# An attention and spectral mixing kernel: the last segment's scores in full-width units, and a new written-out order of all engines' work

## The chip, the cores and the metric

The kernel runs on one core of a Trainium2 chip. A core has a matrix engine (TensorE, PE in the profile, with PEld for its weight loads), a vector engine (VectorE, DVE), an activation engine (ScalarE, ACT), GpSimd (POOL) and SyncE (SP), which here only issues DMA transfers. The engines run side by side, each through its own queue in order, and wait for one another by semaphores. The metric is device time in microseconds (us); lower is better. Before the change the median of three runs is 236.53 us (235.4 to 236.88).

## What is computed

Two branches over the same input x (2048 tokens by 640 features, bf16) are mixed by a sigmoid gate per token. Branch A is attention with 32 heads of 20 features over four segments of 512 tokens. Each segment has causal softmax attention inside itself, and reads from a memory (M, z) that sums the segments before it. Branch B is a two-dimensional Fourier transform, a product with a complex weight, and the inverse transform.

```
for s in range(N):                       # N = 4 segments of L = 512
    qs, ks, vs = (q[:, :, s].copy(), k[:, :, s].copy(), v[:, :, s].copy())
    logits = jnp.einsum('bhqd,bhkd->bhqk', qs, ks) * scale + mask
    p = _softmax(logits, axis=-1)
    a_dot = jnp.einsum('bhqk,bhkd->bhqd', p, vs)
    pq = phi(qs)                         # t + 1 where t > 0, else exp(t)
    a_mem = num / den                    # pq with M, pq with z
    o = g * a_mem + (1.0 - g) * a_dot
    pk = phi(ks)
    M = M + jnp.einsum('bhld,bhle->bhde', pk, vs)
    z = z + jnp.einsum('bhld->bhd', pk)
...
X = rfft2(x); y = irfft2(X * (w_r + 1j * w_i))
out = g * (o @ wo) + (1 - g) * y         # g = sigmoid(sum(x * gate_w))
```

## The kernel before

Everything lies in one program that writes out each engine's instructions. `record` lists the operations with what they read and write; from that come the waits. The order in which each engine runs them is not found when the kernel is built: it stands in the list `ORDER` (L639). An entry is twice the operation's number, plus one where the operation has two engines to choose from and takes the second. `Sched.schedule` deals the entries out to five queues, so `ORDER` sets the order within TensorE, VectorE, ScalarE, GpSimd and SyncE, and which engine a copy (`copy_alts`) or a sum (`either`) runs on. A transfer in SyncE's queue that waits holds all transfers behind it.

Scores. For each segment the 32 heads are eight groups of four (g), two groups a pair (`pr`). The triangle of 512 by 512 scores is split in three kinds of unit, each of which fills four banks of PSUM (2048 columns a partition), is run by `qk_unit` on TensorE in a row-tiled array mode (`mode=1`), and is then exponentiated by ScalarE into the tile `ex`. Kind 0 and kind 1 hold one head group each; kind 2 gathers the small pieces that are left, 128 columns a head. In segments 1 and 2 (`wide`, L1256) a unit of kind 2 gathers those of four groups, every second pair; in segments 0 and 3 it gathers two groups, once in every pair (`UNITS`). Segment 3 has a layout of its own in `ex` (a pitch of 1280 per head where the others have 1088, `exo`, L1317): its exps of kind 1 are written in two parts of 1280 and 768 elements, and those of kind 2 in two parts of 512 (L1352 to L1362).

GpSimd clears what the causal mask forbids (`masks`, `mask`, L1407). In segments 0 to 2 the values are multiplied in a column-tiled mode (`pv_flipped`, `mode=2`), stored in DRAM (`u_scr`), and read back for the output projection. In segment 3 `pv_group` uses the exponentials as weights (L1431 and after), VectorE normalizes (`pv_den`, `pv_rec`, `pv_mul`, L1443 to L1448), the memory term in `mem` is added (`addmem`, L1453), and `last_transposes` turns the result round on TensorE.

Memory. Segments 1 and 2 store what they read from the memory in DRAM (`o_scr`); eight DMA transposes (name `oT`, L600) bring it back as `mT`, four per segment, and `finish_tile` adds them (L1670). `Macc` is the running memory.

Spectral branch. Stages F1, D, T, Tb and Db on TensorE run between the attention parts; Db's results are copied (`ev_Db`, tile `eo`) and summed into `G` (L1617).

Output. `finish_tile` does each of 16 tiles of 128 tokens in two halves: a product of `G` with the gate table `fbg` (Fb, column-tiled), then five output projections into the same bank, and a copy to `ot`, which is stored. The gate table of a segment comes from `gate_table`: a load of `gbc` and one product (L1093). A projection with `mode=-1` is flexible: it is run column-tiled as four products (L565) where its bank is held in that mode. `FLAT` names the halves that are run flat instead.

Array modes of TensorE are thus three: 0 (flat), 1 (row-tiled scores), 2 (column-tiled).

## Time and profile before

| | |
|---|---|
| median of three runs | 236.53 us (235.4 to 236.88) |
| profiled execution | 236.15 us |
| its span, first to last instruction | 234.1 us |
| instructions | 10363 |
| granted TensorE clock | 1.000 |
| moved by DMA | 42.18 MB, mean 180 GB/s |

The span is the time from the first to the last instruction of the profiled execution; 2.05 us lie around it. Views of the trace: the page begins with each engine's busy time. The chain of waits goes back from the last instruction to what released each step. The windows give busy time by stretch. Groups of instructions carry their line, engine, operation, what is written from what (`ex<-psum`), shape, count, busy time and mean length in ns, then the idle time before them. The lines of waits read: who waited, for whom, total us, times, longest. A helper's line stands for many places: L567 and L565 are all matrix products, L602 and L600 all transfers and all DMA transposes, L577 and L579 all copies on ScalarE and VectorE.

### The profile page before, as it was taken

How to read it: one execution, taken by the hardware profiler on the slowest of the kernel's cores; microseconds unless marked ns; L12 is line 12 of the kernel's file. 1: busy time of each engine (PE TensorE's matmuls, PEld its weight loads, DVE VectorE, ACT ScalarE, POOL GpSimd, SP SyncE). 2: the span in 40 equal slices, each digit the busy share in tenths (PEclk: the TensorE clock that was granted, in tenths of full speed). 3: DMA queues.
4: the chain of work that ended last, by engine and by line, in shares of the span. 5: the costliest groups of instructions: out<-in, count | busy, mean ns of one | idle time of the engine just before them, and what ended most of it. 6: DMA issues, size and time to landing. Idle time of an engine off the chain costs nothing.

```text
span 234.1 us, 10363 instructions
## 1 busy us (share of the span) xinstructions
PE 222.8 (95%) x4377; PEld 141.1 (60%) x4391; DVE 190.5 (81%) x483; ACT 196.6 (84%) x231; POOL 152.7 (65%) x303
## 2 busy tenths in 40 slices
PE   7799999999999999999999999999999999999994
PEld 2575676676555666555557545556545467667783
DVE  0389998799999896899999998999799984925564
ACT  2189888888999899999999889999999889898820
POOL 8133138365777777476796467587989677597920
PEclk9999999999999999999999999999999999999999
DMA  7999859999989457968664788577968638416224
GB/s 149 285 345 259 232 152 170 198 224 213 206 193 191 107 161 205 232 127 211 174 168 125 208 238 209 148 204 223 208 166 223 183 108 145 121 34 178 80 88 113
DMA packets 59266, 42.18 MB, mean 180 GB/s; under 512 B 30229, under 2 KB 55381, under 8 KB 59221
## 3 DMA queue, kind: packets, MB, share of 16 engines
q1 hardware_dynamic: 58180, 40.96, 75.1%
q8 instruction: 34, 0.56, 1.0%
q10 hardware_dynamic: 1040, 0.57, 0.9%
q14 instruction: 12, 0.09, 0.1%
HBM read 23.32 MB, written 12.30 MB: 152 GB/s over the span
## 4 chain that ended last, share of the span: by engine, by line
PE 70%; DVE 13%; DMA 7%; ACT 3%; SPq 2%; issue 2%; POOL 1%; DVEq 0%
PE psum L567 62%; PE psum L565 8%; DMA wk<-in_A_wk_dram 3%; DVE Pt L1563 3%; ACT ex L1370 2%; DMA pkn<-phk 2%; DVE G L1617 2%; DMA qkp<-qk_scr 2%; SPq L600 2%; DVE mem L1228 1%; DVE va L1186 1%; DVE ub L579 1%; DVE dnr L1293 1%; DVE dn L1226 1%; DVE Cp L579 1%
## 5 line engine op out<-in xcount | busy, mean ns | idle before, releaser
L1407 POOL TENSOR_SCALAR_AFFINE_SELECT ex<-ex 128x256 bf16<-128x256 bf16 (+3 forms) x224 | 104.2, 484 | 36.8 <-ACT ex L1370 6.9
L1370 ACT ACTIVATE ex<-psum 128x2048 bf16<-128x2048 f32 (+1 forms) x56 | 101.7, 1816 | 6.9 <-PE psum L567 5.5
L1361 ACT ACTIVATE ex<-psum 128x1280 bf16<-128x1280 f32 (+3 forms) x32 | 36.2, 1130 | 5.0 <-PE psum L567 4.4
L567 PE MATMUL psum<-qkp 20*64 20x64 bf16 (+5 forms) x1280 | 32.1, 270 | 1.5 <-ACT ex L1370 0.8
L567 PE MATMUL psum<-xT,wk 128*128 128x256 bf16 (+1 forms) x280 | 32.5, 273 | 0.4 <-DMA wk<-in_A_wk_dram 0.2
L567 PE MATMUL psum<-xT,wq 128*128 128x512 bf16 (+1 forms) x121 | 28.3, 380 | 2.2 <-DMA xT<-in_A_x_dram 1.7
L567 PE MATMUL psum<-wv,xT 128*32 128x321 bf16 (+3 forms) x385 | 26.4, 301 | 0.0
L1563 DVE TENSOR_TENSOR Pt<-psum,Wt 128x642 bf16<-128x642 f32 x32 | 25.6, 822 | 0.4
L567 PEld LDWEIGHTS psum<-xT,wk 128*128 128x128 bf16 (+1 forms) x280 | 20.0, 97 | 7.2 <-issue 1.5
L567 PEld LDWEIGHTS psum<-qkp 20*64 20x64 bf16 x1280 | 13.5, 103 | 17.5 <-ACT ex L1370 10.2
L976 POOL TENSOR_TENSOR xsb<-xf 128x320 bf16<-128x320 bf16 (+2 forms) x11 | 8.1, 743 | 19.8 <-DVE xf L971 10.8
L565 PE MATMUL psum<-wo,oU 128*32 128x320 bf16 x460 | 20.6, 300 | 0.0
L567 PE MATMUL psum<-big,Cp 128*128 128x321 bf16 (+1 forms) x96 | 19.0, 303 | 0.5 <-DVE G L1617 0.2
L567 PE MATMUL psum<-big,Ac 128*128 128x161 bf16 (+2 forms) x96 | 18.3, 258 | 0.4 <-DVE va L1186 0.2
L579 DVE CAST ot<-psum 128x320 bf16<-128x320 f32 x16 | 7.5, 491 | 13.0 <-PE psum L565 9.9
L567 PEld LDWEIGHTS psum<-wv,xT 128*32 128x32 bf16 (+1 forms) x385 | 13.4, 96 | 6.7 <-issue 1.4
L567 PE MATMUL psum<-ex,va 128*32 128x64 bf16 (+3 forms) x576 | 17.2, 256 | 0.3 <-ACT qu L577 0.3
L1617 DVE TENSOR_TENSOR G<-eo,psum 128x320 bf16<-128x320 f32 x32 | 15.0, 480 | 2.9 <-PE psum L567 2.6
L1186 DVE TENSOR_TENSOR va<-psum,ebx 128x320 bf16<-128x320 f32 x32 | 15.3, 486 | 2.2 <-PE psum L567 1.0
L567 PE MATMUL psum<-tt,Yt 128*128 128x256 bf16 (+1 forms) x96 | 16.2, 275 | 0.7 <-DVE Yt L1568 0.2
L567 PEld LDWEIGHTS psum<-ex,va 128*32 128x32 bf16 x576 | 10.8, 96 | 8.6 <-POOL ex L1407 1.5
L1143 ACT ACTIVATE et<-qu 128x512 bf16<-128x512 bf16 x25 | 15.7, 626 | 0.0
(106 smaller groups left out, 408.6 us busy)
## 6 DMA issues: line engine op xcount, KB each, us to landing
qkp<-qk_scr SPq DMA_DIRECT2D x28, 160.0 KB
tt<-tab_tt SPq DMA_DIRECT2D x8, 512.0 KB, 4.5
qk_scr<-qu SPq DMA_DIRECT2D x12, 256.0 KB, 3.6
u_scr<-ub SPq DMA_DIRECT2D x12, 256.0 KB, 3.5
xsb<-in_A_x_dram SPq DMA_DIRECT2D x8, 320.0 KB, 6.1
oU<-u_scr SPq DMA_DIRECT2D x15, 128.0 KB, 3.7
out_dram<-ot SPq DMA_DIRECT2D x12, 160.0 KB
Wt<-in_B_w_r_dram SPq DMA_DIRECT2D x16, 80.2 KB, 2.6
```

The source lines that it names most:

```text
L565: h = e.matmul(dst, wt, r_, start=st, stop=sp_, **{**kw, "tile_position": (0, q), "skip_group_check": True})
L567: h = e.matmul(o_, l_, r_, start=st, stop=sp_, **kw)
L579: alts["dve"] = (lambda e: e.tensor_copy(dst(), src()), 67 + 1.04 * n, 68.0)
L600: return e.dma_start_transpose(d_, s_)
L976: self.either(lambda e, dst=dst, src=src, d0=d0, n=n, op=op: e.tensor_tensor(xs.ap(o + dst, [D, 2], [1, n]), xf.ap(src + d0, [321, 2], [1, ...
L1143: self.one("act", lambda e: e.activation(et.ap(0, [1, L]), qsl(), ACT.Exp), L, [qb], [b("et", pi_)], late, fix=95, name="phi_exp")
L1186: self.one("dve", lambda e: e.tensor_tensor(va.ap(i * H * VW + h0 * VW, [VW, nh], [1, DH]), self.ps(bank, 0, [DH, nh], [1, DH]), self.ebx. ...
L1361: self.one("act", lambda e, d=d, q=q: e.activation(self.ex.ap(*d), self.ps(bank, *q), ACT.Exp, scale=SC), (2048, (1280, 768)[x], 512)[kind ...
L1370: self.one("act", lambda e, d=d, q=q: e.activation(self.ex.ap(*d), self.ps(bank, *q), ACT.Exp, scale=SC), 2048 if kind < 2 else 512 * n, [ ...
L1407: self.one("pool", lambda e: e.affine_select(self.ex.ap(*d, p0=p0, np_=np_), self.ex.ap(*q, p0=p0, np_=np_), [[0, 4], [1, n]], ALU.is_ge, ...
L1563: self.one("dve", lambda e, ri=ri, Pt=Pt, Wt=Wt, wo_=wo_, bank=bank: e.tensor_tensor(Pt.ap(ri * 322, [644, 2], [1, KD]), self.ps(bank, 0, ...
L1617: self.one("dve", lambda e, q=q, n2=n2, bank=bank, eo=eo: e.tensor_tensor(self.G.ap(n2 * D + 639 * q, [1 - 2 * q, 320]), eo.ap(q, [1, 320] ...
```

## The change

- `wide` is true for segment 3 and for the second half (two pairs) of segment 0, so that their kind 2 units gather four head groups.
- Segment 3 takes the layout of the other segments (`exo`, `EPITCH`). Its exps are written whole, one per unit. The small pieces of groups 4 to 7 and a new piece of `ex` (`X2COL`, keys x2 and x2c, one block of 128 columns per head in three turns) take over SBUF that `ub` and `Macc` had; the first writer there waits for their users (`home`, and `after` in `mask`).
- The masks of segment 3 are as many as before, three per group on the small pieces; two of the seven write out of place into the new piece.
- `pv_group` takes its weights from the new places and waits for the new keys.
- `FLAT` names one other half tile.
- `ORDER` is replaced: its first entries differ by the operations' new numbers alone, then they stand in another order. It has 2311 entries, 2329 before. In it the eight `oT` transposes come at entries 120, 161, 164, 172, 183, 191, 195 and 196 of SyncE's 239; before at 160, 161, 171, 181, 185, 188, 206 and 218. The gate store and gate load of the last segment come at 222 and 227; before at 207 and 219. Some operations change engine, among them four `ev_Db` copies from ScalarE to VectorE and four `addmem` from GpSimd to VectorE.

```diff
--- before.py
+++ after.py
@@ -639,101 +639,101 @@
     ORDER = (
...
-        264, 304, 80, 306, 368, 106, 308, 82, 266, 104, 370, 84, 268, 1622, 66, 270, 132, 372, 272, 386, 87, 310, 570, 274, 313, 388, 280, 572, 68,
+        264, 304, 80, 306, 368, 106, 308, 82, 266, 104, 370, 84, 268, 1618, 66, 270, 132, 372, 272, 386, 87, 310, 570, 274, 313, 388, 280, 572, 68,
...
@@ -811,7 +811,7 @@
         self.wo = [T(f"wo{c}", [P, D], at=self.pkn.off + 1280 * c if c < 4 else self.et[0].off) for c in range(5)]
         self.oU += [T("oU1", [P, 5 * L], at=self.phq.off), T("oU2", [P, 5 * L], at=self.va[0].off)]
         self.NEX = 3
-        self.ex = T("ex", [P, self.ONCOL + 4 * D])
+        self.ex = T("ex", [P, self.X2COL + 3 * 4 * P])
         self.cur = self.ex.off + 2 * self.ONCOL
         self.on = T("on", [P, 4 * D])
         self.mem = T("mem", [P, 4 * D])
@@ -822,6 +822,7 @@
         self.rc = T("rc", [P, P])
         self.gcc = T("gcc", [P, P], F32)
         self.Macc = T("Macc", [P, 880], F32)
+        assert self.ub[0].off == self.ex.off + 2 * self.UBCOL and self.Macc.off == self.ex.off + 2 * self.X2COL
         self.Mz = [T(f"Mz{i}", [P, 880]) for i in range(2)]
         self.hm = T("hm", [P, 880])
         self.beta = T("beta", [P, H])
@@ -1236,7 +1237,7 @@
     def attend(self, s):
         b = self.b
         for pr in range(4):
-            if self.wide(s):
+            if self.wide(s, pr):
                 units = (((0, 1, 2, 3), 2),) * (pr % 2 == 0) + (((0,), 0), ((0,), 1), ((1,), 0), ((1,), 1))
             else:
                 units = self.UNITS
@@ -1253,8 +1254,8 @@
         if s < 3:
             self.denominators(s)
-    def wide(self, s):
-        return s in (1, 2)
+    def wide(self, s, pr):
+        return s > 0 or pr > 1
     def pv_flipped(self, s, g):
@@ -1301,30 +1302,27 @@
     EBASE = 4 * 512
     MBASE = EBASE + 3 * 4 * 1088
     ONCOL = MBASE + 512
+    UBCOL = ONCOL + 2 * 4 * D
+    X2COL = UBCOL + 4 * L + 4 * P
     def exb(self, s, g, k):
-        if s == 3:
-            return self.b("ex3", g % 3, k)
+        if s == 3 and (k[0] == "x" or k == "c0" and g > 3):
+            return self.b("ex3", g % 3 if k[0] == "x" else g, k)
         if k == "c0":
             return self.b("exc", g)
         return self.b("ex", (s * 8 + g) % 3, k)
-    def ex3(self, g):
-        b = self.b
-        e = lambda x: [b("ex", x, k) for k in ("a0", "b0", "m1")]
-        return ([b("exc", x) for x in range(4)] + e(0), e(0) + e(1), e(1) + e(2) + [b("ex", x, "m3") for x in range(3)])[g]
-
     def exo(self, s, g):
-        return g % 3 * 5120 if s == 3 else self.EBASE + ((s * 8 + g) % 3) * 4 * self.EPITCH
+        return self.EBASE + ((s * 8 + g) % 3) * 4 * self.EPITCH
     def exc(self, s, g):
-        return 512 * g if g < 4 else self.MBASE + 768 + 512 * (g - 4)
+        return 512 * g if g < 4 else (self.UBCOL if s == 3 else self.MBASE + 768) + 512 * (g - 4)
     def exm(self, s, g):
         return self.MBASE + (s * 8 + g) % 3 * 256
     def exall(self, s, g):
-        return [self.exb(s, g, k) for k in ("a0", "b0", "c0", "m1", "m3") + ("b1",) * (s == 3)]
+        return [self.exb(s, g, k) for k in ("a0", "b0", "c0", "m1") + (("m3",) if s < 3 else ("x2", "x2c"))]
     def qk_unit(self, s, pr, u, unit):
         self.Sc.group += 1
@@ -1349,26 +1347,15 @@
         g = 2 * pr + gps[0]
         ks = "abc"[kind]
         e0, n = self.exo(s, g), len(gps)
-        if s == 3:
-            step = self.exo(s, g + 1) - e0 if kind == 2 else 0
-            if kind == 0:
-                outs = [((e0, [1280, 4], [1, 512]), (0, [512, 4], [1, 512]))]
-            elif kind == 1:
-                outs = [((e0 + 576, [1280, 4], [1, 320]), (0, [512, 4], [1, 320])), ((e0 + 960, [1280, 4], [1, 192]), (320, [512, 4], [1, 192]))]
-            else:
-                outs = [((e0 + 896 + x * step, [1280, 4], [320, 2], [1, 64]), (x * 128, [512, 4], [64, 2], [1, 64])) for x in range(2)]
-            for x, (d, q) in enumerate(outs):
-                self.one("act", lambda e, d=d, q=q: e.activation(self.ex.ap(*d), self.ps(bank, *q), ACT.Exp, scale=SC), (2048, (1280, 768)[x], 512)[kind], [bank],
-                         [self.exb(s, 2 * pr + (x if kind == 2 else gp), ks + str(x * (kind == 1))) for gp in gps], prio - self.QK_LEAD, name="exp" + str(x)[x == 0:],
-                         after=[q for gp in gps if 2 * pr + gp < 3 for q in self.ex3(2 * pr + gp)])
+        if kind == 2:
+            d, q = (self.exc(s, g), [128, 4], [512, n], [1, 128]), (0, [512, 4], [128, n], [1, 128])
         else:
-            if kind == 2:
-                d, q = (self.exc(s, g), [128, 4], [512, n], [1, 128]), (0, [512, 4], [128, n], [1, 128])
-            else:
-                d, q = (e0 + 576 * kind, [self.EPITCH, 4], [1, 512]), (0, [512, 4], [1, 512])
-            home = [b("xf", k) for k in range(3)] if s == 0 and kind == 2 and pr > 1 else []
-            self.one("act", lambda e, d=d, q=q: e.activation(self.ex.ap(*d), self.ps(bank, *q), ACT.Exp, scale=SC), 2048 if kind < 2 else 512 * n, [bank],
-                     [self.exb(s, 2 * pr + gp, ks + "0") for gp in gps], prio - self.QK_LEAD, name="exp", after=home)
+            d, q = (e0 + 576 * kind, [self.EPITCH, 4], [1, 512]), (0, [512, 4], [1, 512])
+        home = [b("xf", k) for k in range(3)] if s == 0 and kind == 2 and pr > 1 else []
+        if s == 3 and kind == 2 and pr > 1:
+            home = [b("ub", k, x) for k in range(2) for x in range(2)]
+        self.one("act", lambda e, d=d, q=q: e.activation(self.ex.ap(*d), self.ps(bank, *q), ACT.Exp, scale=SC), 2048 if kind < 2 else 512 * n, [bank],
+                 [self.exb(s, 2 * pr + gp, ks + "0") for gp in gps], prio - self.QK_LEAD, name="exp", after=home)
         if kind < 2:
             for gp in gps:
                 self.masks(s, 2 * pr + gp, ks, prio)
@@ -1376,29 +1363,26 @@
     def masks(self, s, g, ks, prio):
         e0, c0, m0 = self.exo(s, g), self.exc(s, g), self.exm(s, g)
-        ep = [1280 if s == 3 else self.EPITCH, 4]
+        ep = [self.EPITCH, 4]
         cp = [P, 4]
-        if s < 3:
-            if ks == "a":
-                self.mask(s, g, P, (e0 + 512, ep), (e0, ep), 64, ("a0",), ("m1",), prio, 64)
-                self.mask(s, g, P, (e0, ep), None, P, (), ("a0",), prio, 0)
-            elif ks == "b":
-                self.mask(s, g, 64, (e0 + 512, ep), None, P, (), ("b0", "m1"), prio, -64)
-                self.mask(s, g, P, (e0 + 896, ep), None, 64, (), ("b0",), prio, 64)
-            else:
-                self.mask(s, g, 64, (m0, [64, 4]), (c0, cp), 64, ("c0",), ("m3",), prio, 0, 64)
-                self.mask(s, g, P, (c0, cp), None, 64, (), ("c0",), prio, 0)
-                self.mask(s, g, 64, (c0 + 64, cp), None, 64, (), ("c0",), prio, 0)
-        elif ks == "a":
+        x0 = self.X2COL + g % 3 * 4 * P
+        if ks == "a":
             self.mask(s, g, P, (e0 + 512, ep), (e0, ep), 64, ("a0",), ("m1",), prio, 64)
             self.mask(s, g, P, (e0, ep), None, P, (), ("a0",), prio, 0)
         elif ks == "b":
             self.mask(s, g, 64, (e0 + 512, ep), None, P, (), ("b0", "m1"), prio, -64)
-            self.mask(s, g, P, (e0 + 960, ep), None, 64, (), ("b1",), prio, 64)
+            if s < 3:
+                self.mask(s, g, P, (e0 + 896, ep), None, 64, (), ("b0",), prio, 64)
+            else:
+                self.mask(s, g, P, (x0 + 64, cp), (e0 + 896, ep), 64, ("b0",), ("x2",), prio, 64)
+        elif s == 3:
+            self.mask(s, g, P, (x0, cp), (c0, cp), 64, ("c0",), ("x2c",), prio, 0)
+            self.mask(s, g, 64, (c0, cp), None, 64, (), ("c0",), prio, 0, 64)
+            self.mask(s, g, 64, (c0, cp), None, P, (), ("c0",), prio, -64)
         else:
-            self.mask(s, g, P, (e0 + 1152, ep), (e0 + 896, ep), 64, ("c0",), ("m3",), prio, 64)
-            self.mask(s, g, P, (e0 + 896, ep), None, 64, (), ("c0",), prio, 0)
-            self.mask(s, g, 64, (e0 + 1152, ep), None, P, (), ("c0", "m3"), prio, -64)
+            self.mask(s, g, 64, (m0, [64, 4]), (c0, cp), 64, ("c0",), ("m3",), prio, 0, 64)
+            self.mask(s, g, P, (c0, cp), None, 64, (), ("c0",), prio, 0)
+            self.mask(s, g, 64, (c0 + 64, cp), None, 64, (), ("c0",), prio, 0)
     def mask(self, s, g, np_, d, q, n, rk, wk, prio, base, p0=0):
@@ -1406,7 +1390,8 @@
         q = d if q is None else (*q, [1, n])
         self.one("pool", lambda e: e.affine_select(
             self.ex.ap(*d, p0=p0, np_=np_), self.ex.ap(*q, p0=p0, np_=np_), [[0, 4], [1, n]], ALU.is_ge, 0.0, base=base, channel_multiplier=-1), 4 * n,
-            [self.exb(s, g, k) for k in rk], [self.exb(s, g, k) for k in wk], prio, per=0.793, fix=218, name="mask")
+            [self.exb(s, g, k) for k in rk], [self.exb(s, g, k) for k in wk], prio, per=0.793, fix=218, name="mask",
+                 after=[self.b("Macc", t) for t in range(5)] * (wk[0][0] == "x"))
         self.Sc.ops[-1].part = p0 > 0
     def pv_group(self, s, g):
@@ -1417,13 +1402,13 @@
         G = s * 8 + g
         e0 = self.exo(s, g)
+        c0, x0 = self.exc(s, g), self.X2COL + g % 3 * 4 * P
+
         def weights(hh, i, jj):
-            o = e0 + hh * 1280
-            if jj == 0:
-                return self.ex.ap(o + i * P, [1, P])
-            if jj == 1:
-                return self.ex.ap(o + 512 + (i - 1) * P, [1, P])
-            return self.ex.ap(o + 896 + (i - 2) * P if jj == 2 else o + 1152, [1, P])
+            o = e0 + hh * self.EPITCH
+            if jj < 2:
+                return self.ex.ap(o + jj * 512 + (i - jj) * P, [1, P])
+            return self.ex.ap(c0 + hh * P if jj == 3 else x0 + hh * P if i == 2 else o + 960, [1, P])
         if True:
             prio = self.texp(s, g, 3 + g % 2) + self.PV_LAG
             bank = Bank(1, "gen")
@@ -1436,7 +1421,7 @@
                                     weights(hh, i, jj),
                                     va.ap(jj * H * VW + (4 * g + hh) * VW, [1, DH + 1]), jj == 0, jj == i, {})
                         items.append((th, 22))
-                self.mms(items, [self.exb(s, g, k) for k in (("a0",), ("a0", "b0", "m1"), ("a0", "b0", "b1", "c0", "m1"), ("a0", "b0", "b1", "c0", "m1", "m3"))[i]] + [b("va", s % 2, jj) for jj in range(i + 1)] + [bank], [],
+                self.mms(items, [self.exb(s, g, k) for k in (("a0",), ("a0", "b0", "m1"), ("a0", "b0", "m1", "x2", "x2c"), ("a0", "b0", "c0", "m1"))[i]] + [b("va", s % 2, jj) for jj in range(i + 1)] + [bank], [],
                          prio, name="pv")
             rs, rsb = self.rs[G % 4], b("rs", G % 4)
             dgb = b("dg", G % 4)
@@ -1635,7 +1620,7 @@
             self.Sc.op(self.copy_alts(lambda c=c: self.oTl.ap(c * L, [1, L]), lambda bank=bank: self.ps(bank, 0, [1, L]), L),
                        r=[bank], w=[b("oTl", c)], prio=prio, name="ev_oT3", after=[b("wqa"), b("wqb")])
-    FLAT = ((1, 0, 1),)
+    FLAT = ((0, 2, 0),)
     def finish_tile(self, s, a):
```

186 rows, old and new, of the table ORDER are left out of this document.

## The prediction

> **What bounds the kernel now.** I read the page first: the busy shares, then the chain that ended last.
>
> ```profile
> PE 222.8 (95%) x4377; PEld 141.1 (60%) x4391; DVE 190.5 (81%) x483; ACT 196.6 (84%) x231; POOL 152.7 (65%) x303
> ...
> PE 70%; DVE 13%; DMA 7%; ACT 3%; SPq 2%; issue 2%; POOL 1%; DVEq 0%
> ```
>
> TensorE is busy for 222.8 of 234.1 us and carries 70% of the chain. VectorE carries 13%, more than ScalarE (3%), although ScalarE is busier. Next the busy time by stretch, since an average over stages says little (columns: TensorE, weight loads, VectorE, ScalarE, GpSimd, clock, DMA share, GB/s).
>
> ```profile
> 0.00:12.00 12.00, 9.02 (x142) 4.61 (x142) 2.61 (x6) 1.88 (x2) 6.71 (x11) 1.00 0.90 221
> 12.00:40.00 28.00, 27.60 (x418) 18.93 (x413) 25.36 (x71) 24.64 (x38) 11.93 (x22) 1.00 1.00 234
> 40.00:190.00 150.00, 145.28 (x2647) 87.80 (x2656) 138.29 (x346) 140.30 (x153) 106.62 (x222) 1.00 0.82 186
> 190.00:220.00 30.00, 29.97 (x898) 20.18 (x890) 16.70 (x46) 26.10 (x35) 23.69 (x44) 1.00 0.48 121
> 220.00:230.00 10.00, 10.00 (x296) 8.98 (x292) 6.54 (x16) 3.69 (x6) 3.79 (x7) 1.00 0.25 80
> 230.00:234.10 4.10, 0.93 (x28) 0.64 (x20) 1.02 (x3) 0.00 (x0) 0.00 (x0) 0.97 0.51 139
> ```
>
> There are three regimes. Up to 40 us loads and the first projections set the pace. From 40 to 190 us TensorE idles 150 - 145.28 = 4.7 us, while VectorE (138.3) and ScalarE (140.3) are nearly full, so all three engines touch there. From 190 to 230 us, where the last segment and the output projections run, TensorE idles 0.03 us; ScalarE has 30 - 26.1 = 3.9 us to spare up to 220 and VectorE 13.3. There only TensorE's own work counts.
>
> What does TensorE lose inside its busy time? The waits of its weight loads, in the columns total us, times, longest:
>
> ```profile
> PEld psum L567 <- issue: 13.4, 59, 0.3
> PEld psum L567 <- ACT ex L1370: 10.2, 37, 0.6
> PEld psum L567 <- DVE Pt L1563: 3.4, 12, 0.6
> PEld psum L567 <- ACT ex L1361: 2.8, 11, 0.3
> ```
>
> Most are many waits of one size (13.4/59 = 0.23, 10.2/37 = 0.28, 2.8/11 = 0.25 us), whatever releaser is named. The timeline shows where they stand:
>
> ```profile
> 206.68 0.16 PEld L567 LDWEIGHTS psum<-qkp 20*64 20x64 bf16 x12 [0.27 <-ACT ex L1361]
> ...
> 207.03 0.26 PEld L565 LDWEIGHTS psum<-wo,oU 128*32 128x32 bf16 x12 [0.20 <-issue]
> ```
>
> They stand where TensorE goes from one array mode to another: output projection (column-tiled) to score unit (row-tiled), 0.27 us, and back, 0.20 us. The exp named for the first is ScalarE's previous one, not a late one: its result frees a bank just as the unit is due.
>
> **The change part by part.** The sum is made against the profiled execution: 236.15 us, that is a span of 234.1 and 2.05 around it. The median of the runs shown is 236.53, 0.38 above, so I carry the difference over to the median.
>
> (1) Score units. The last segment goes from 20 units to 18 (two units of small pieces over four head groups replace four over two), the second half of the first segment from 10 to 9: 76 to 73 in all. The same matmuls run, so no TensorE work goes but the entries and exits. To see what the new ORDER does, I gave each TensorE entry of both lists the mode that its helper passes (1 for scores, 2 for column-tiled, 0 for flat, the flexible ones that of their bank's group) and counted neighbours of different mode: 210 before, 205 after. The one flat output projection that moves (FLAT) is in that count. Four of the five removed switches lie where the list corresponds to 190 to 220 us (30 to 26), one between 40 and 90 (48 to 47). At 0.20 us each, the lower of the two rows above, that is 5 x 0.20 = -1.0 us: 0.8 in a stretch where nothing else can hold TensorE, 0.2 where a wait may take its place. Bounds: 5 x 0.27 = -1.35, and 0 if the neighbours' matmuls cover the gap.
>
> The Trainium skill (TensorEngine Tiling, section Key Properties) says that changing the tiling mode drains TensorE. The rows above agree, and give the price that the page lacks.
>
> (2) Exps. The rows that price them, and the operations that change engine:
>
> ```profile
> L1370 ACT ACTIVATE ex<-psum 128x2048 bf16<-128x2048 f32 x52 | 97.6, 1877 | 6.8 <-PE psum L567 5.5
> L1361 ACT ACTIVATE ex<-psum 128x2048 bf16<-128x2048 f32 x8 | 15.0, 1877 | 2.6 <-PE psum L567 2.5
> L1361 ACT ACTIVATE ex<-psum 128x1280 bf16<-128x1280 f32 x8 | 9.9, 1237 | 0.9 <-PE psum L567 0.8
> L1361 ACT ACTIVATE ex<-psum 128x768 bf16<-128x768 f32 x8 | 6.5, 810 | 0.2
> L1361 ACT ACTIVATE ex<-psum 128x512 bf16<-128x512 f32 x8 | 4.8, 597 | 1.2 <-PE psum L567 1.1
> L1370 ACT ACTIVATE ex<-psum 128x1024 bf16<-128x1024 f32 x4 | 4.1, 1024 | 0.2
> L577 ACT ACTIVATE eo<-psum 128x321 f32<-128x321 f32 x10 | 4.2, 438 | 0.2 <-PE psum L567 0.2
> L579 DVE COPY eo<-psum 128x321 f32<-128x321 f32 x6 | 2.9, 487 | 0.2 <-PE psum L567 0.2
> L1453 POOL TENSOR_TENSOR on<-on,mem 128x320 bf16<-128x320 bf16 x4 | 3.2, 790 | 0.3 <-DVE on L1448 0.3
> L1453 DVE TENSOR_TENSOR on<-on,mem 128x320 bf16<-128x320 bf16 x4 | 1.4, 372 | 0.1
> ```
>
> Last segment: 15.0 + 9.9 + 6.5 + 4.8 = 36.2 us in 32 exps become 18 x 1.877 = 33.8 (-2.4). First segment: 2 x 1.024 become 1.877 (-0.2). On the path both count 0: ScalarE had 3.9 us to spare there. ScalarE's slack is the cover, and the change makes it larger.
>
> (3) Engine choices in ORDER. ScalarE gives VectorE four copies of the spectral output (-4 x 0.438 = -1.8, +4 x 0.487 = +1.9), and a net two of the final copies of about the same length. GpSimd gives VectorE three memory additions in `on` (-3 x 0.790, +3 x 0.372) and one in `oU`. So VectorE gains about 4.5 us, most of it after 165 us. After 190 us its 13.3 us of slack cover it; the copies at 167 to 190 us do not have that cover. I take 0, with +1.9 as the upper end (all four copies exposed).
>
> (4) Masks. Their number stays (7 per group). Two of the seven now write into a new piece of `ex`, where `Macc` lay, and the small pieces of groups 4 to 7 lie where `ub` was. The added waits are on those old users (the last memory update, the last stores to `u_scr`), which ORDER puts ahead of them. GpSimd has 30 - 23.69 = 6.3 us to spare at 190 to 220: 0.
>
> (5) SyncE. It issues the same 239 transfers, so no DMA is added; only their order changes. The eight transposed loads of the stored memory term stand at entries 120 to 196 of its queue, 160 to 218 before. Each holds SyncE for 1.25 to 2.2 us:
>
> ```profile
> L600 SPq DMA_TRANSPOSE mTx<-o_scr x4: 1253/1586/2163, 143.8 to 166.9; - x4
> L600 SPq DMA_TRANSPOSE mT<-o_scr x3: 1258/1260/1284, 163.7 to 196.2; - x3
> ```
>
> What they feed is needed after 188 us and TensorE hardly waited for it, so early loads gain 0; the last, issued at 196.2, was the one near its use. They are moved past weights of the spectral part, past `pkn` transposes and past the score operands (`qkp`), each of which goes out up to 2.2 us later if it was tight. In the other direction go the gate store and gate load of the last segment: entries 222 and 227, 207 and 219 before (a rival, below).
>
> (6) The rest of the reordering, 40 to 190 us, can give back up to the 4.7 us of idle time found above or add to it. No row prices that, and neither sign is favoured: VectorE and ScalarE remain nearly full there. I take 0, nearest to what the equal work of all engines says.
>
> Sum: 236.15 - 1.0 = 235.15 for the profiled execution, 236.53 - 1.0 = 235.5 for the median.
>
> **The rivals.**
>
> The order fills the holes. If half of the 4.7 us goes as well: 235.5 - 2.4 = 233.1. For it: that idle time is in many short waits, and ScalarE has 5 us less to do. Against: VectorE, not ScalarE, carries the chain there.
>
> The saving does not show. The gap at a switch is covered by a bank that is not free anyway, or the copies added to VectorE eat it: 236.5. For it: the wait named at the gap is an exp.
>
> The last gate table comes too late (slower). In the new order its load is behind three output stores, and on VectorE its product stands between the normalizing steps of the last two head groups, directly ahead of the matmuls (`Fb`) that open the last eight output tiles. Before, there was ample room:
>
> ```profile
> 198.55 0.35 SPq L602 DMA_DIRECT2D gbc<-g_scr  x1
> ```
> ```profile
> 213.16 0.80 DVE L1093 TENSOR_TENSOR fbg<-fcat,gbc 128x512 bf16<-128x512 bf16 x1
> ```
> ```profile
> DMA to landing us min/median/max: 3.6/4.2/4.8
> ```
> ```profile
> SPq L602 <- DVE ot L579: 13.1, 3, 5.7
> SPq L602 <- ACT ot L577: 10.3, 3, 6.8
> ```
>
> From issue to use 14.6 us passed, with 3.6 to 4.8 of them for the landing. After the change I place the issue at about 215.6 and the product at about 222.5, so some 6.9 us, by counting the entries along the mean times of their kinds. A store ahead that waits 2.1 us longer than planned (6.9 - 4.8) uses this up; from there each us is lost whole, since VectorE's queue behind holds the last normalization. Stores wait up to 6.8 us in that stretch: at worst 6.8 - 2.1 = +4.7, 240.2.
>
> A transposed load stops SyncE. The first stands 5 entries behind the last store of the segment that it reads back (36 before). If SyncE stands there as long as it stood for TensorE at most elsewhere, operands behind it are late:
>
> ```profile
> SPq L602 <- PE psum L567: 16.5, 12, 4.2
> ```
>
> With 1.2 us of room by my placing, 4.2 - 1.2 = +3.0: 238.5.
>
> An addition on VectorE waits for a mask. A mask takes 0.63 us at most; four moved additions are 4 x 0.63 = +2.5 at worst, 238.0. The rows show the reverse order only, masks waiting for additions:
>
> ```profile
> POOL ex L1407 <- DVE oU L1670: 1.5, 2, 1.0
> ...
> POOL ex L1407 <- DVE on L1453: 0.8, 1, 0.8
> ```
> ```profile
> L1407 POOL TENSOR_SCALAR_AFFINE_SELECT ex<-ex 128x512 bf16<-128x512 bf16 x32 | 20.1, 632 | 2.9 <-DVE rc L1295 1.4 <-DVE phk L1155 0.5 <-ACT Bt L577 0.4
> ```
>
> The Trainium skill (SBUF — State Buffer, section Who interferes with whom) has this as a rule: a VectorE instruction with two SBUF inputs and a GpSimd one that reads SBUF exclude each other, and the one issued first blocks the other. The trace agrees on one side only, so the chance is small.
>
> **How the numbers follow.** Switches saved, rest neutral (235.5): 0.40, with its own range 234.3 to 236.9. Holes filled (233.1): 0.24. Saving hidden (236.5): 0.18. Gate table late (up to 240.2): 0.10. SyncE stopped (238.5): 0.05. Additions blocked (238.0): 0.03. A measurement of this kernel can tell about 1% from no change: under 234.2 is faster, over 238.9 slower. Faster: nearly all of the second case, 0.24. Slower: most of the late gate table and, if its 3.0 is exceeded, SyncE stopped, together with longer stalls of the reordered middle (0.05 out of the hidden saving): 0.17. Same: 0.59. The range 232.4 to 239.0 leaves out the worse part of the gate case (0.08) and what lies beyond half of the holes (0.08).
>
> **What would show it.** Right: 73 score units; between 190 and 230 us TensorE still without idle time but done about 0.8 us earlier; ScalarE at about 191 us in all, VectorE at about 195. The gate rival shows as VectorE waiting for `gbc` near 222 us and TensorE for `fbg`; the SyncE rival as a wait at L600 near 109 us; the holes as TensorE idle clearly under 4.7 us from 40 to 190. The prediction is wrong if TensorE has new waits over 0.5 us there, or if the switches cost as much in fewer places.

## The result, and the profile after

After the change the median is 237.86 us (ten runs) where the kernel before takes 236.55: a ratio of 1.006, 95% interval 1.003 to 1.009. All ratios leave out executions more than 1.5% above the fastest of the same kernel: one of these ten, and five of the twelve of the kernel after in a0, all of them with a mean granted clock under 0.992. Measured again beside its variants (a0 below) it was 1.008, interval 1.004 to 1.013. The time lies in the range that was given, on the other side of no change from the forecast 235.5: the gain of 1.0 us became a loss of 1.3. The profiled execution took 237.12 us, with a span of 235.3, 1.2 longer than before.

The page of the kernel after, busy shares and chain:

```profile
PE 224.1 (95%) x4391; PEld 141.2 (60%) x4391; DVE 192.0 (82%) x492; ACT 192.3 (82%) x210; POOL 148.3 (63%) x300
...
PE 69%; ACT 9%; DVE 7%; DMA 6%; POOL 3%; SPq 3%; issue 2%; DVEq 0%; POOLq 0%
```

ScalarE is 4.3 us shorter, about as reckoned, and VectorE 1.5 longer, where 4.5 were reckoned; yet ScalarE's share of the chain rises from 3% to 9%. The busy time by stretch (columns as before):

```profile
40.00:190.00 150.00, 145.60 (x2635) 86.19 (x2628) 135.91 (x344) 137.49 (x145) 105.98 (x225) 1.00 0.79 189
190.00:220.00 30.00, 29.57 (x878) 21.11 (x878) 19.57 (x54) 24.88 (x23) 20.62 (x39) 1.00 0.38 108
220.00:230.00 10.00, 10.00 (x299) 8.81 (x292) 6.16 (x17) 3.86 (x6) 2.96 (x6) 1.00 0.21 68
230.00:235.30 5.30, 2.08 (x64) 1.79 (x56) 2.31 (x6) 0.00 (x0) 0.00 (x0) 1.00 0.47 124
```

Two things are to be seen. From 190 to 220 us TensorE, which had idled 0.03 us there, now idles 0.43. And past 230 us it still has 64 matmuls to do (28 before): it comes to its end 1.15 us later (232.08 against 230.93). What it idles in all is the same (235.3 - 224.1 = 11.2, before 234.1 - 222.8 = 11.3), so the loss hides in its busy time, as gaps before weight loads.

To find it I laid the two traces' TensorE operations beside the two lists (4391 weight loads in each), gave each operation the time from its start to the next one's, and called the 30th percentile of that time, over all operations of the same kind, mode and following mode in six traces, its work. What is above it is wait.

| kernel | mode switches | work, us | waits, us | TensorE done at |
|---|---|---|---|---|
| before | 210 | 205.5 | 24.1 | 230.9 |
| after | 205 | 205.1 | 25.6 | 232.1 |
| f1 (more switches) | 224 | 208.5 | 23.7 | 233.5 |
| s1b (new units, old order) | 205 | 205.3 | 32.2 | 238.8 |
| m1 (three switches fewer) | 207 | 204.8 | 26.0 | 232.1 |
| m5 (seven fewer) | 203 | 204.0 | 26.8 | 232.1 |

From before to after the work falls by 0.4 us and the waits grow by 1.5: +0.3 up to 40 us, +1.2 from 40 to 60, -0.5 to 100, +0.8 from 100 to 110, -0.9 from 110 to 190, +0.7 behind 190. Each row is a single execution: m1 and m5, which are the kernel before unchanged up to 183 and 140 us, differ from it by up to 0.7 us in the parts behind 40 us. Halved clock is in two rows: in m1 from 7.6 to 11.0 us (its waits ahead of 40 us are 1.5 above those of before), in s1b from 203.6 to 210.4 us. Three single waits of the kernel after are new. The weight loads around the first, and around the third:

```profile
45.19 0.47 PEld L567 LDWEIGHTS psum<-qkp 20*64 20x64 bf16 x48
45.70 0.61 PEld L567 LDWEIGHTS psum<-ex,va 128*32 128x32 bf16 x24
46.24 1.10 PEld L567 LDWEIGHTS psum<-wv,xT 128*32 128x32 bf16 x35
49.15 0.11 PEld L567 LDWEIGHTS psum<-wv,xT 128*32 128x32 bf16 x5 [1.81 <-issue]
```
```profile
197.05 0.20 PEld L567 LDWEIGHTS psum<-qkp 20*64 20x64 bf16 x22 [0.27 <-ACT ex L1357]
197.74 0.23 PEld L567 LDWEIGHTS psum<-qkp 20*64 20x64 bf16 x26 [0.50 <-issue]
```

"issue" names no releaser. My reading is that the instructions themselves were not there. The first wait stands 59 loads behind a gathered unit (48 products and 48 loads in 0.5 us), the second inside one; a 16 KB block of instructions was on its way in both cases (the queue of instruction blocks, 46.5 to 47.8 us and 195.3 to 196.4), and TensorE went on 1.3 to 1.4 us after it had landed. All traces together bear this out. The 34 such blocks stand against 8782 loads and products, some 258 to a block, and the waits keep to fixed places in that stream: of the twenty traces, eleven (m1 in the old order is one) have a wait of TensorE for "issue" of over 0.3 us that ends at the 727th weight load, and eleven one that ends at the 3384th or next to it, whatever product stands there. Of all 30 such waits behind 20 us, 29 end 1.2 to 1.6 us after a block has landed. The second new wait, on VectorE and then on TensorE:

```profile
103.90 0.29 DVE L1156 TENSOR_SCALAR phk<-qu 128x512 bf16<-128x512 bf16 x1 [1.20 <-DMA pkn<-phk]
```
```profile
105.22 0.41 PE L567 MATMUL psum<-tt,Yt 128*65 128x256 bf16 x2 [1.00 <-DVE Bt L579]
```

VectorE writes `phk` again while the transposed load that reads it is still out (issued at 98.18, 5.7 us), and the copy of `Bt` stands behind. The gate table of the last segment, my slower rival, came in time, and VectorE did not wait for it (6.6 us from issue to use; a load of this table lands 3.7 us after its issue):

```profile
217.07 0.51 SPq L602 DMA_DIRECT2D gbc<-g_scr  x1
```
```profile
223.63 0.68 DVE L1094 TENSOR_TENSOR fbg<-fcat,gbc 128x512 bf16<-128x512 bf16 x1
```

### The profile page after: what moved, and what is told of

Same layout as the page of the kernel before. It is cut to its first block, busy times and chain, and to the rows that moved or that the text cites. A ratio compares the mean times of both kernels' runs of the same rounds, so it can differ in the third digit from the quotient of the medians.

```text
span 235.3 us, 10359 instructions
## 1 busy us (share of the span) xinstructions
PE 224.1 (95%) x4391; PEld 141.2 (60%) x4391; DVE 192.0 (82%) x492; ACT 192.3 (82%) x210; POOL 148.3 (63%) x300
## 4 chain that ended last, share of the span: by engine, by line
PE 69%; ACT 9%; DVE 7%; DMA 6%; POOL 3%; SPq 3%; issue 2%; DVEq 0%; POOLq 0%
PE psum L567 61%; PE psum L565 7%; ACT ex L1357 7%; DMA beta<-in_A_beta_dram 3%; DMA pkn<-phk 2%; DVE Pt L1548 2%; POOL ex L1391 2%; SPq L600 2%; SPq L602 1%; ACT et L1144 1%; DVE Bt L579 1%; DVE Cp L579 1%; DVE ub L579 1%; POOL fbg L1094 0%; DVE Macc L1467 0%
## 5 line engine op out<-in xcount | busy, mean ns | idle before, releaser
L1357 ACT ACTIVATE ex<-psum 128x2048 bf16<-128x2048 f32 (+1 forms) x73 | 135.2, 1852 | 13.6 <-PE psum L567 12.3
L567 PE MATMUL psum<-xT,wk 128*128 128x256 bf16 (+1 forms) x280 | 33.7, 273 | 0.3 <-ACT q L577 0.3
L567 PE MATMUL psum<-xT,wq 128*128 128x512 bf16 (+1 forms) x135 | 31.8, 381 | 1.4 <-DMA xT<-in_A_x_dram 1.4
L567 PE MATMUL psum<-wv,xT 128*32 128x321 bf16 (+3 forms) x385 | 26.8, 301 | 1.5 <-issue 1.5
L565 PE MATMUL psum<-wo,oU 128*32 128x320 bf16 x460 | 19.8, 299 | 0.0
L567 PE MATMUL psum<-tt,Yt 128*128 128x256 bf16 (+1 forms) x96 | 16.8, 276 | 1.6 <-DVE Bt L579 1.2
L567 PE MATMUL psum<-big,Cp 128*128 128x321 bf16 (+1 forms) x96 | 17.9, 302 | 0.2
L567 PE MATMUL psum<-big,Ac 128*128 128x161 bf16 (+2 forms) x96 | 17.2, 257 | 0.0
L579 DVE CAST ot<-psum 128x320 bf16<-128x320 f32 x18 | 8.5, 490 | 10.2 <-PE psum L565 7.3
L972 DVE TENSOR_TENSOR xf<-xsb 128x640 bf16<-128x640 bf16 x16 | 8.1, 513 | 8.5 <-DMA xsb<-in_A_x_dram 8.5
```

The source lines that it names most:

```text
L565: h = e.matmul(dst, wt, r_, start=st, stop=sp_, **{**kw, "tile_position": (0, q), "skip_group_check": True})
L567: h = e.matmul(o_, l_, r_, start=st, stop=sp_, **kw)
L579: alts["dve"] = (lambda e: e.tensor_copy(dst(), src()), 67 + 1.04 * n, 68.0)
L972: self.either(lambda e, r=r, op=op: e.tensor_tensor(xf.ap(r * 642, [321, 2], [1, 320]), xs.ap(o, [D, 2], [1, 320]), xs.ap(o + 320, [D, 2], ...
L1357: self.one("act", lambda e, d=d, q=q: e.activation(self.ex.ap(*d), self.ps(bank, *q), ACT.Exp, scale=SC), 2048 if kind < 2 else 512 * n, [ ...
```

## The experiments

Ratios are to the kernel before, run beside each on the same chip, with 95% intervals. My first theory was that the order costs (above all SyncE's), the rivals that the units or the moved engine choices do.

**The parts of the change taken alone.** s1b has the new units in the old order:

```diff
-    FLAT = ((0, 2, 0),)
+    FLAT = ((1, 0, 1),)
     ORDER: that of before on every engine; a unit over four groups
     stands where the earlier of its two former units stood
```

> The new units in the old order: the last segment has 18 full-width units and half of the first segment 9, each two-group unit standing where the earlier of its two former units stood; every other operation on every engine, SyncE's queue and the flat output projection stay as in the kernel before. 205 mode switches by the same count, as after. If the order is what costs (my first theory), the loss of after is gone: 235.5 to 236.5 us, and the five switches are worth 1.0 us by the prediction, 0.3 by the alignment of the two traces. If the units themselves cost (the gathered unit holds all four banks of the scores for 1.88 us, where small exps freed them sooner), it stands at 237 to 238.

Measured: 1.040 (1.036 to 1.043), 245.2 us. Both theories missed. By 190 us it is 1.9 us behind before, 1.2 of them in one wait at 63 us for the longer exp of the gathered unit; then the last segment breaks down:

```profile
203.18 0.46 PE L567 MATMUL psum<-va,ex 128*128 128x21 bf16 x12 [2.98 <-POOL ex L1390]
```
```profile
201.64 1.48 POOL L1390 TENSOR_SCALAR_AFFINE_SELECT ex<-ex 64x512 bf16<-64x512 bf16 x3 [2.12 <-DVE oU L1644]
```
```profile
200.15 1.42 DVE L1644 TENSOR_TENSOR oU<-oU,r 128x512 bf16<-128x512 bf16 x4
```

The products wait for masks, and these begin 0.07 us after four multiplications of VectorE end. That wait is the program's own: `Sched.schedule` gives a GpSimd operation a wait for the VectorE operation marked `lock` that it places ahead of it (`o.dyn.append(ldv)`, L257 of the kernel before), and the first of these masks has one for the last of the four. The wait takes s1b from 1.7 to 5.4 us behind before; a further 1.7 go in the 6.8 us of halved clock that follow, and all six runs of s1b have a mean clock of 0.984 to 0.986. The new units do not fit the old order.

s2 is after with SyncE's queue in the old order:

```diff
     ORDER: the 239 SyncE entries of before, all else of after
```

> The kernel after, with only SyncE's queue put back into the order of before (the same 239 transfers). If the order of the loads is what costs, 236.3 to 236.9 us, and the wait of TensorE for Bt near 104 us (1.3 us, behind a 5.7 us wait for pkn) is gone. If the units or the order of the engines cost, 237.5 to 238.

Measured: 1.047 (1.041 to 1.053). The new order needs its loads when the new queue brings them: TensorE waits 1.6 us for `qkp` at 205 us alone. In its profiled execution the clock was halved twice besides, for 3.4 us each (from 140.2 and from 211.9 us).

s4 is after with the old engine choices:

```diff
     ORDER: after's; 35 entries changed to the engine they had before
```

> The kernel after with its order, but each operation that changed engine back on the engine that it had before (35: among them the four copies of the spectral output and four memory additions leave VectorE). If VectorE's added 4.5 us are what costs (the upper end that I gave them, +1.9), 236 to 236.8 us. If they lie under other work, as the prediction took, 237.5 to 238.3.

Measured: 1.020 (1.015 to 1.025), slower than after. The operations given to VectorE are not the loss; within the new order that choice helps.

**The price of a switch.** f1 is before with another flat half tile:

```diff
-    FLAT = ((1, 0, 1),)
+    FLAT = ((2, 1, 0),)
```

> The kernel before with another output projection of the first three segments as the flat one (segment 2, group 1, first half), all orders unchanged: 224 mode switches by count against 210, the same matmuls. At the 0.20 us of the prediction 14 switches are +2.8 us: 239.3. At the 0.07 that the alignment of the two traces gives (0.33 us for five) +0.9: 237.5. If neighbours cover a switch, 236.6.

Measured: 1.011 (1.008 to 1.014), +2.4 us over the median beside it: 2.4 / 14 = 0.17 us a switch, and 0.21 in work by the table. The price of 0.20 was right for these.

**The single waits of after, removed one at a time.** c1 moves work ahead of the first, c2 VectorE's write behind the copy, c3 work ahead of the third, c4 all three:

```diff
 TensorE (c1)
+F1, proj x5
 qk gathered, pvf, vproj x10
-F1, proj x5
 VectorE (c2)
-write to phk
 write to phq x2, ev_D
+write to phk
 TensorE (c3)
+Db x3
 qk gathered, pv
-Db x3
```

> The kernel after, with one move on TensorE: six operations with long matmuls (one F1, five projections of two matmuls, 12 weight loads and about 1.0 us of work) go from just behind the dense stretch at 43.7 to 47.2 us to just ahead of the gathered unit in it. Theory (instruction supply): the 1.47 us wait at 47.68 is TensorE waiting for its next instruction block, which comes at a fixed time near 49.15; work put ahead of it is done inside the wait, so the wait shrinks by about 1.0 to some 0.5 us, and the time falls by up to 1.0: 236.9. Rival (the wait only takes the place of waits that follow anyway, since both kernels reach that instruction at 49.15): the wait shrinks, but the time stays at 237.5 to 238.2.

> The kernel after, with one move on VectorE: the write to phk that stands waiting for the transposed load pkn<-phk at 103.90 us (1.2 us) goes three operations later, behind the two for phq and the copy of Bt. If VectorE's place for it is what makes TensorE wait 1.0 us for Bt at 105.2, that wait goes to under 0.3 us and the time to about 237.0. If the load behind it sets the pace, the wait moves to the next user and the time stays at 237.5 to 238.2.

> The kernel after, with one move on TensorE: three matmuls of the spectral part (Db, 0.14 us each) go from behind the gathered unit at 197.05 us to just ahead of it; one mode switch more by count (206). By the theory of instruction supply the wait of 0.50 us at 197.74 shrinks by about 0.4; with the switch (0.2) the net is -0.2, so 237.3 to 237.9. The trace decides: if that wait stays at 0.5, it is not a matter of how many instructions stand ahead of it.

> The kernel after with the three moves together. If each wait is lost time of its own, they add: -1.0 - 0.9 - 0.2, some 235.6 to 236.0 us, and the kernel stands no longer above the one before (236.4). If waits only move, 237 to 238.

Measured: c1 1.008 (1.005 to 1.012), c2 1.011 (1.004 to 1.018), c3 1.013 (1.007 to 1.020), c4 1.017 (1.012 to 1.021). None gives time back, and c4, where the three moves together should have gained 2 us, is the slowest. In c1 the wait at 47 us is gone and its place taken:

```profile
48.52 1.77 PE L567 MATMUL psum<-wv,xT 128*32 128x321 bf16 x36 [0.67 <-DVE ub L579]
```

In c2 the wait for `Bt` is gone, and one that after does not have comes at 156 us, as in c1 and c3, for a table whose load stands behind a transposed load in SyncE's queue (columns of the second fence: start, length, issue):

```profile
156.22 0.44 PE L567 MATMUL psum<-Bt,tt 128*128 128x321 bf16 x2 [1.08 <-DMA tt<-tab_tt]
```
```profile
148.41 1.30 SPq L600 DMA_TRANSPOSE mTx<-o_scr  x1
149.75 0.59 SPq L602 DMA_DIRECT2D wo<-in_A_wo_dram  x1
150.38 0.60 SPq L602 DMA_DIRECT2D tt<-tab_tt  x1
```

In c3 the third wait is still there (0.64 us in an execution of 243.3 us), three products earlier in the gathered unit, that is, at the same 3384th weight load. With other products ahead of that place the wait stays:

```profile
201.65 0.35 PE L567 MATMUL psum<-qkp 20*64 20x128 bf16 x29 [0.64 <-issue]
```

**SyncE and the first segment.** a0 is after itself; d1 moves the eight transposed loads back, d2 only the table ahead of one of them, d3 undoes the gathering in the first segment:

```diff
 SyncE (d1): the eight oT entries where before has them
 SyncE (d2)
+ld_tt (last)
 oT, ld_wo
-ld_tt (last)
 d3
-        return s > 0 or pr > 1
+        return s > 0
```

> The kernel after, unchanged, beside its variants on one chip. By its first measurement the ratio to the kernel before is 1.006 (1.003 to 1.009): 237.9 us where before takes 236.5.

> The kernel after, with only its eight transposed loads of the stored memory term moved back in SyncE's queue, each to the place that it has in the kernel before, measured in TensorE work (entries 120 to 196 become 158 to 216); everything else as in after. If the early transposed loads hold up loads behind them (the theory that SyncE's order costs), 236.5 to 237.2. If they cost nothing (the prediction: 0), 237.5 to 238.2. If something needs them early (the memory read in the last segment), over 238.5.

> The kernel after, with the last load of the table tt (512 KB) moved ahead of one transposed load and two weights in SyncE's queue, so that it goes out about 2 us earlier than at 150.26 us. In three variants of after TensorE waited 0.8 to 1.1 us for this table near 156 us. If those 2 us are missing, that wait is gone and the time 0.5 to 1.0 us under after. If the table is only sometimes late, or its buffer comes free later, the time is that of after.

> The kernel after with one part undone: the second half of the first segment has its two units of small pieces over two groups again (74 score units), both at the place of the gathered one; the last segment and the order stay. If the gathered unit's 96 short instructions in 0.5 us are what runs TensorE out of instructions at 47.68 us, that wait shrinks by 0.5 us or more, since the second unit has to wait for the first one's exp. If the units themselves are neutral, the time is that of after, or up to 0.3 us above it for the added exp; under after by 0.5 or more if this part of the change costs.

Measured: a0 1.008 (1.004 to 1.013), d1 1.015 (1.009 to 1.020), d2 1.007 (1.003 to 1.011), d3 1.010 (1.006 to 1.014). The early transposed loads are not the loss: put back, they give nothing back (that they then cost is not clear of the noise, since the intervals of d1 and a0 overlap). d2 has no wait for `tt`, as meant, and the time of after. d3 has neither the wait at 47 us nor that at 104 (its second small unit waits 1.3 us for the exp of the first instead), and it reaches the same projection at 195.4 us as after at 195.3. Then, up to 210 us, it loses 2.2 us more than after, and d2 1.5, in a way that after's own profile does not show. Stretches of d3, then of after:

```profile
195.00:200.00 5.00, 4.41 (x165) 3.50 (x158) 2.28 (x7) 4.14 (x4) 3.47 (x7) 1.00 0.34 93
200.00:205.00 5.00, 5.00 (x118) 3.47 (x118) 4.49 (x15) 2.86 (x4) 2.92 (x4) 0.54 0.69 203
205.00:210.00 5.00, 5.00 (x120) 3.15 (x116) 3.25 (x9) 3.40 (x3) 1.49 (x5) 0.77 0.14 49
```
```profile
195.00:200.00 5.00, 4.62 (x173) 3.67 (x166) 2.58 (x8) 4.34 (x4) 3.24 (x7) 1.00 0.28 78
200.00:205.00 5.00, 4.95 (x150) 3.87 (x151) 4.83 (x16) 3.77 (x4) 3.33 (x5) 1.00 0.67 200
```

The clock granted to TensorE is halved (0.54 over 200 to 205 us), behind the gathered unit and its wait of 0.59 us for instructions. A mean clock under 0.998 over the whole execution, which does not tell the place, was recorded in 9 of 22 runs of after, in 4 of the 29 of before beside a0 and in 17 of all 85 of before beside the variants. The six runs of after's first measurement that had the full clock have a median of 237.48, so some 0.9 of its 1.3 us is there without the clock. Beside a0 the runs at full clock have medians of 238.63 (after, seven) and 236.82 (before, 25): there 1.8 us are lost without the clock.

**Further, since the cause was open.** g1 is d3 with the second small unit 14 us later; h1 gathers in the first segment in the old order; k4 puts flat projections behind the last segment's gathered unit; g2 is g1 with k4:

```diff
 g1
-        return s > 0 or pr > 1
+        return s > 0
 h1 (kernel before)
-        return s in (1, 2)
+        return s in (1, 2) or s == 0 and pr > 1
 k4
-    FLAT = ((0, 2, 0),)
+    FLAT = ((0, 2, 0), (1, 0, 0))
```

> The kernel after with one part undone: the second half of the first segment has its two units of small pieces over two groups again, the first at the place of the gathered unit, the second some 14 us later beside another small one, where ScalarE has time (74 score units, 207 switches by count); last segment and order stay. If the gathered unit of the first segment is what costs (the two waits of TensorE of 1.8 and 1.1 us at 47 and 104 us went when it was taken apart, but the second unit then waited for the first one's exp), 1.0 to 1.5 us under after, near the kernel before. If those waits only take the place of others, the time of after. In either case the clock near 200 us should halve in as many runs as with after, since the last segment is the same.

> The kernel before with one part done alone: the second half of the first segment gathers its small pieces (75 score units), the gathered unit at the place of the first of the two, and the three units behind it moved back by one exp; the last segment and every other order as before. If gathering by itself is neutral and only the new order costs, the time of before within 0.3 per cent. If it costs by itself, 0.4 per cent or more above. The clock near 200 us should stay at 1.0.

> The kernel after with five output projections flat (1 weight load each in place of 4) and three of them moved from ahead of the gathered unit at 197 us into the small products behind it. In the traces of the variants of after, TensorE's clock halves for 3 to 7 us from about 200 to 208 us, behind this unit, in some runs, and with it 1.7 to 2.3 us go. If the clock halves because the stretch behind the unit is too thin (short waits and tiny products), fuller work there keeps it at 1.0 in nearly all runs, and the median comes down by 0.5 to 1.0 us. If the clock has another cause, as many runs show it as with after (9 of 22 by their mean clock).

> Both edits together: the pairs of the first segment taken apart and spread, and the flat projections behind the gathered unit of the last. If both theories hold, 1.5 to 2.2 us under after and at or just under the kernel before (ratio 0.996 to 1.002). If neither holds, the ratio of after, 1.006 to 1.008.

Measured: g1 1.020 (1.014 to 1.026), h1 1.027 (1.021 to 1.033), k4 1.026 (1.020 to 1.032), g2 1.029 (1.022 to 1.035). All are worse than after. g1 met the late table (1.7 us at 156). In h1 a full exp of 1.88 us stands where one of 1.02 did, and ScalarE's copies behind it come late:

```profile
69.93 0.35 PE L567 MATMUL psum<-Mz,phq 128*128 128x154 bf16 x3 [0.92 <-ACT qu L577]
...
80.64 1.08 PE L567 MATMUL psum<-ex,va 128*32 128x512 bf16 x24 [1.03 <-POOL ex L1407]
```

Behind each of these two waits the clock was halved for 3.4 us (from 70.6 and from 80.9 us); but h1's one run at full clock took 240.66 us, where before takes 236.6. So h1 does not clear the unit: in this place of the old order it costs by itself (its three moved followers included). In k4 all six runs had a mean clock under 0.998: the flat projections did not keep it up, and my theory of the clock (too thin a stretch) has nothing for it.

**Switches taken away in the old order.** m1 and m5 move operations of TensorE in the kernel before, and nothing else:

```diff
 TensorE (m1, m5)
 Db 1 of a tile
+Db 2, Db 3
 Fb, oproj
-Db 2
 oproj, oproj, Fb, oproj, Fb
-Db 3
 TensorE (m5 besides)
+vproj                    two places earlier
+pvf of the third segment  eight places earlier, behind the other one
```

> The kernel before with three mode switches fewer (207 by count) and nothing else: in TensorE's queue two single matmuls (Db) that stand alone between output projections at 183.45 and 184.48 us go up to 1.8 us earlier, behind the other one of their tile. At the 0.20 us of the prediction 3 switches are 0.6 us: 235.9 where before takes 236.5. At 0.06 (the alignment of the traces for the five that the change removes) 0.2: no difference. If the two come before their operands, TensorE waits and it is slower.

> The kernel before with seven mode switches fewer (203 by count): the two moves of the run beside it, one value projection two places earlier, and one of the products pvf of the third segment from 168.5 us to just behind the other one, some 1.5 us earlier. At 0.20 us 7 switches are 1.4 us: 235.1 (ratio 0.994). At 0.06 0.4 us: 236.1. The pvf may wait for its masks; then less, or slower.

Measured: m1 1.001 (0.997 to 1.004), m5 1.010 (1.006 to 1.015). The work falls as priced, by 0.7 and 1.5 us (0.23 and 0.22 a switch), and no gain shows (m1's interval still holds 0.6 us). The trace of m1 says why. From one Db ahead of the moves (at 179.38 us before, 180.62 in m1) to one behind them (186.69 and 187.85) it takes 7.31 us before and 7.23 in m1, 0.08 less where the price says 0.6. Its weight loads, m1:

```profile
183.43 0.15 PEld L567 LDWEIGHTS psum<-qkp 20*64 20x64 bf16 x12 [0.27 <-ACT ex L1361]
...
185.48 0.10 PEld L567 LDWEIGHTS psum<-G,fbg 128*32 128x32 bf16 x4 [0.23 <-DVE G L1617]
185.89 0.16 PEld L567 LDWEIGHTS psum<-qkp 20*64 20x64 bf16 x12 [0.31 <-ACT ex L1361]
```

and before:

```profile
182.19 0.15 PEld L567 LDWEIGHTS psum<-qkp 20*64 20x64 bf16 x12 [0.27 <-ACT ex L1361]
...
184.23 0.10 PEld L567 LDWEIGHTS psum<-G,fbg 128*32 128x32 bf16 x4
...
184.72 0.16 PEld L567 LDWEIGHTS psum<-qkp 20*64 20x64 bf16 x12
```

Two score units stand 2.53 us apart before and 2.46 in m1. The second may not start before the exp of the first (1.88 us) has freed the banks. That exp, first in m1, then before:

```profile
183.96 1.88 ACT L1361 ACTIVATE ex<-psum 128x2048 bf16<-128x2048 f32 x1 [0.36 <-PE psum L567]
```
```profile
182.71 1.88 ACT L1361 ACTIVATE ex<-psum 128x2048 bf16<-128x2048 f32 x1 [0.36 <-PE psum L567]
```

It ends at 185.84 and 184.59, and the unit follows 0.05 and 0.13 us later. No unit in either trace follows its exp by less than 0.05, so 0.08 us was all the room there was; the rest of what the switches saved becomes a wait for `G` (0.23) and for that exp (0.31). m5 waits besides: the moved `pvf` 0.72 us for its operands at 167 us, a Db 0.65 at 169.8.

## Why the prediction was wrong

- **Step (1) failed, twice.** The count 210 to 205 and the price of 0.20 are right for projections (f1: 0.17 to 0.21; m1, m5: 0.22). But the removed switches are those of units of small pieces, and these were worth 0.4 us in all, 0.08 each (s1b: 0.05): by the laid-out traces a unit over two groups (24 products and their 24 loads) takes 0.247 us with its way out and the gathered one (48 and 48) takes 0.509, so leaving the mode adds nothing that shows, and only three ways in are saved. And the ground for "0.8 in a stretch where nothing else can hold TensorE" does not hold. That TensorE has no idle time in the page does not say that it sets the pace: score units and exps take turns over the same four banks, and the next unit waits. m1 shows it in the old order just ahead of 190 us: 0.08 of 0.6 us arrived. Behind 190 there was more room: in the trace of before the twelve units there begin 0.05 to 0.32 us after the exp ahead of them, which leaves 1.4 us in all above the least value of 0.05. In after the eleven units there begin 0.19 to 0.41 us after it, so what holds them there is what stands ahead of them on TensorE, not the exp.
- **Step (2)**, exps: 73 and ScalarE at 192.3, as said. "On the path both count 0" holds for the sum of exp time, but the slack of 3.9 us was no cover for a longer single exp: in s1b and h1 a full exp where a short one stood holds up copies, masks and the next unit.
- **Step (3)**, VectorE: 192.0 us, I said 195. That it costs nothing holds: with the operations moved back it was slower (s4).
- **Step (4)**, masks: no wait of TensorE for them above 0.3 us stands in after; in the old order (s1b) masks were the largest wait, and it was a wait that the program makes itself. So are the three waits of masks for additions that the prediction took as the trace's agreement with a rule of the chip: `schedule` adds just three such waits to the kernel before. They neither agree with the rule nor speak against it.
- **Step (5)**, SyncE: right for the transposed loads (d1: put back, they give no gain), and the gate came in time. "Goes out up to 2.2 us later if it was tight" came true for the table `tt`, for which TensorE does not wait in after but waits 0.8 to 1.7 us in five variants (c1, c2, c3, g1, g2).
- **Step (6)** put the new order at nothing without a price: "can give back up to 4.7 us or add to it", taken as 0. Between 40 and 190 us the waits grew by some 0.5 net, with single ones of 1.8 and 1.1 us. Behind 190, where no step had a term for the order, they grew by 0.7. With the work down by only 0.4, these waits are the loss. My own sign of a wrong prediction, new waits over 0.5 us there, is what the trace shows.
- **The rivals.** The nearest was that the saving does not show (236.5), for the reason that it named: a bank that is not free anyway. That reason is shown only ahead of 190 us. No rival had the supply of instructions or the clock.

What stays open: which of the order's many waits makes up the 0.9 to 1.8 us that are lost at full clock. Twelve variants of after took back single waits or parts, and none was faster than after by more than its interval; no version here beats before. That the order as a whole is tied to its units, loads and engines is shown (s1b, s2, s4); that another order for the new units would gain is not.

## What to carry to other kernels

Where a written-out order keeps several engines full, a saving on one of them counts only as far as the next wait: follow the stretch to the next operation that waits for another engine before a removed gap is booked as time. Do not take a tuned order apart to see what its parts are worth without expecting each part to cost by itself, and measure a price by adding much of the same kind (f1, +14) rather than by taking little away: f1's 0.17 us was not the price of the switches that this change removed.

## What the runs showed of the hardware

TensorE can outrun its instructions. In after it waited 1.5 and 0.4 us between products with no releaser, behind and inside a gathered score unit (96 instructions in 0.5 us); such waits stand at the same weight loads (727th, 3384th) in eleven traces each and end 1.2 to 1.6 us after a 16 KB instruction block has landed.

Its clock can be halved for a while in the middle of a busy kernel: in d3 for 6.8 us (from 200.4 to 207.3 us), after a stretch in which it idled only 0.59 of 5 us. Between 20 and 230 us every such stretch in the twenty traces lasts 3.4 or 6.8 us. The Trainium skill (TensorE: Matmul & The Clock Gate, HAM oscillation) speaks of idle gaps above some 3.4 us for that; here the clock fell after 0.59 us of idle time in d3, and stayed full in c2 after 1.94 us of it in 3.4 (from 46.0 to 49.4 us). What decides it stays open.
